# Two plain float32 products in place of nine bfloat16 ones as TensorE's warm-up, in a gated mix of a long convolution and an MLP

## The chip, the core and the metric

One core of a Trainium2 chip runs the whole program in one launch. The metric is the device time in microseconds (us). The kernel before takes 385.71 us, the median of three runs that lie between 385.69 and 385.95.

## What is computed

The inputs are x (2048 rows of 512), k and v of the same shape, four shift taps and a long filter of 2048 taps for each of the 512 channels, two MLP weights (512 x 1792 and 1792 x 512) and a gate vector of 512.

```python
x = A_q
g = _sigmoid((x * gate_w).sum(-1, keepdims=True))
a = _A_ref(x, A_k, A_v, A_shift_k, A_ssm_k, A_ssm_D)   # 4 taps on k, times v, 2048-tap causal convolution by FFT, + D * kv, times x
b = _B_ref(x, B_w1, B_w2)                              # relu(x @ w1) @ w2
return g * a + (1 - g) * b
```

The warm-up products are no part of this. They multiply ones by ones into a bank of PSUM that nobody reads.

## The kernel before

The MLP is done with operands that are each split into a high and a low part of the type float32r, three products for each tile (high by high, high by low, low by high). A product is 128 x 128 weights by 128 x 512 moving elements. The long convolution is done as a transform over small tiles of TensorE's array, in plain float32: `stage1` (L459) forward, `conv_mid` (L575) and `inverse` (L652) in the middle, `conv_end` (L727) last. The MLP runs in two eras of seven blocks of the hidden dimension, each over four chunks of 512 rows, and the pieces of the convolution are put between the MLP's.

Every piece of work is an operation in a list (`add`) with an engine, a rough duration, a rank and what it depends on. `Plan.order` plays the list through once, at build time, and writes the instructions in the order in which it would start them. So a duration in the list can move instructions on any engine. The hardware then runs each engine's instructions in that order, and semaphores hold an instruction until its operands are there.

The operations around the change are the first ones of the program:

- `warm` (L749 to L753) issues nine bfloat16 products of constant ones, one behind the other. In the list it is one operation of TensorE with the rank (-3,), that takes one of the eight PSUM banks ("cv") and gives it back.
- `load_first` (L317) brings the first four weight blocks in, one for each quarter k of the contraction. The block for k = 0 comes in two halves on ACT's queue (L329), is rounded to its high part by ACT (L334: `w0h_h_g`) and to its low part by DVE (L337: `w0l_l_g`). The blocks for k = 1 to 3 come on SP's queue and have L299 and L302.
- `load_x` brings the first 512 rows of x in; DVE makes the high part for k = 0 and all the low parts (`xh_h`, `xl_l`), ACT the other high parts.
- `mlp1_first` (L354) has the first real products (L362): twelve for each k, in groups that follow the order in which the operands come in. For k = 0 these are two of the high weights' first half by xh, two by xl, the same four for the second half, and four of the low weights by xh.

```python
        first = [(0, n, f) for m in range(2) for n in range(2) for f in (2 * m, 2 * m + 1)] + [(0, 2, f) for f in range(G)]
```

Of the kernel before, what the change touches and what calls it, by code (L numbers as in the profile page):

```python
# [8 lines left out]
F32 = mybir.dt.float32  # L9
# [4 lines left out]
S, D, DFF = 2048, 512, 1792  # L14
P = 128
# [51 lines left out]
def _flat(r):  # L67
    for x in r if isinstance(r, tuple) else (r,):
        yield from _flat(x) if isinstance(x, tuple) else (x,)


class Plan:
# [5 lines left out]
    def add(self, eng, dur, rank, fn, deps=(), take=(), give=(), dma=0, fifo=(), tiles=False, port=False, alt=None, pair=0, soon=False, ends=False):  # L78
        rank = tuple(_flat(rank))
        op = dict(tiles=tiles, alt=alt, port=port or eng == "POOL" and not dma, eng=eng, dur=dur, rank=rank, fn=fn, take=tuple(take), give=tuple(give), dma=dma, fifo=tuple(fifo),  # L80
                  pair=pair, soon=soon, ends=ends or soon, wait=0, next=[], asked=0.0, n=len(self.ops), rest=(), member=False)
        op["fn"] = fn if alt is None else lambda: fn(op["eng"])
        for d in deps:
            if d is not None:
                d["next"].append(op)
                op["wait"] += 1
        for q in fifo:
            self.turn.setdefault(q, []).append(op["n"])
        self.ops.append(op)
        return op  # L90
# [152 lines left out]
MM = 0.227  # L243
# [5 lines left out]
def build(tc, wf, xp, qn, kn, vn, hn, dn, sh, gw, w1, w2, cs1, ccf, cci, cib, out):  # L249
    nc = tc.nc  # L250
# [18 lines left out]
    add = plan.add  # L269
# [8 lines left out]
    def bank(key, tag="cv"):  # L278
        T[key] = pm.tile([P, D], F32, tag=tag, bufs=room0[tag], name="_".join(map(str, key)))
        return T[key]  # L280
# [467 lines left out]

    def warm():  # L749
        ps = bank(("warm",))  # L750
        one = nc.const_aps.tensor(1.0, (P, D), mybir.dt.bfloat16)
        for _ in range(WARM):
            mm(ps, one[:, :P], one, start=True, stop=True)  # L753

    w = add("PE", WARM * 2 * MM / 2, (-3,), warm, (), ["cv"], ["cv"])
    for k in range(4):
        load_x(0, 0, k, -1000 + k)
        load_first(k, -1002.5 + k)
# [59 lines left out]
PATIENCE = 0.5  # L818
BEHIND = 2
G = 4  # L820
WARM = 9
DMA_AHEAD = 2.0
DMA_RATE = 300000.0
DMA_LAG = [0.575, 0.8]
# [66 lines left out]
```

## Time and profile before

| | |
|---|---|
| median of three runs | 385.71 us |
| the profiled execution | 385.97 us |
| its span, first to last instruction | 384.2 us |
| TensorE busy | 379.8 us, 99% of the span |
| VectorE (DVE) busy | 266.7 us, 69% |
| ScalarE (ACT) busy | 128.8 us, 34% |
| mean granted TensorE clock | 0.999 |

The span is what the trace covers; the 1.77 us between it and the profiled execution's time lie outside the instructions. Times in the trace count from the span's start. In the rows PE is TensorE's products, PEld its weight loads, which run beside products, and a name such as `w0h_h_g` is a tile. A product's recorded duration is longer than the distance to the next one, since products follow each other in a pipeline: the distance from start to start is what a product costs.

### The profile page before, as it was taken

How to read it: one execution, taken by the hardware profiler on the slowest of the kernel's cores; microseconds unless marked ns; L12 is line 12 of the kernel's file. 1: busy time of each engine (PE TensorE's matmuls, PEld its weight loads, DVE VectorE, ACT ScalarE, POOL GpSimd, SP SyncE). 2: the span in 40 equal slices, each digit the busy share in tenths (PEclk: the TensorE clock that was granted, in tenths of full speed). 3: DMA queues.
4: the chain of work that ended last, by engine and by line, in shares of the span. 5: the costliest groups of instructions: out<-in, count | busy, mean ns of one | idle time of the engine just before them, and what ended most of it. 6: DMA issues, size and time to landing. Idle time of an engine off the chain costs nothing.

```text
span 384.2 us, 6567 instructions
## 1 busy us (share of the span) xinstructions
PE 379.8 (99%) x2505; PEld 273.8 (71%) x2505; DVE 266.7 (69%) x356; ACT 128.8 (34%) x242; POOL 91.5 (24%) x77
## 2 busy tenths in 40 slices
PE   9999999999999999999999999999999999999996
PEld 5888788668877788788655765565587788688684
DVE  4698999797989028114799687897872347687691
ACT  5643524573147525533224022313400333012100
POOL 0000000000000000000199968866995001000000
PEclk9999999999999999999999999999999999999999
DMA  7997893898648763589867876686460798399331
GB/s 274 368 317 255 298 351 113 293 333 323 208 121 330 295 234 109 185 296 275 285 203 238 307 265 227 241 308 232 139 204 3 241 342 320 120 325 357 117 124 56
DMA packets 43474, 92.51 MB, mean 241 GB/s; under 512 B 4625, under 2 KB 7201, under 8 KB 43442
## 3 DMA queue, kind: packets, MB, share of 16 engines
q1 hardware_dynamic: 43090, 91.77, 68.8%
q8 instruction: 20, 0.33, 0.4%
q10 hardware_dynamic: 288, 0.26, 0.2%
q14 instruction: 12, 0.10, 0.1%
q0 software_dynamic: 64, 0.05, 0.0%
HBM read 61.66 MB, written 30.41 MB: 240 GB/s over the span
## 4 chain that ended last, share of the span: by engine, by line
PE 99%; DVE 0%; DVEq 0%; issue 0%
PE m L406 14%; PE m L407 13%; PE m L408 13%; PE m L376 13%; PE m L377 12%; PE m L378 12%; PE iv L652 4%; PE f_h L575 4%; PE f_x L575 4%; PE m L362 3%; PE s1x L459 2%; PE s1h L459 2%; PE cy L727 2%; PE warm L753 1%; DVE o L677 0%; DVEq L887 0%
## 5 line engine op out<-in xcount | busy, mean ns | idle before, releaser
L623 POOL TENSOR_TENSOR p<-p,ha 128x512 f32<-128x512 f32 x32 | 41.1, 1308 | 202.2 <-DVE ha L617 201.6
L406 PE MATMUL m<-w1h_h,hh 128*128 128x512 f32 x224 | 88.7, 396 | 0.0
L407 PE MATMUL m<-w1l_l,hh 128*128 128x512 f32 x224 | 87.3, 390 | 0.0
L408 PE MATMUL m<-w1h_h,hl 128*128 128x512 f32 x224 | 87.2, 389 | 0.0
L389 ACT ACTIVATE hh<-m 128x512 fp32r<-128x512 f32 x56 | 33.1, 598 | 126.4 <-PE m L378 122.1
L392 DVE SCALAR_TENSOR_TENSOR hl<-m,hh 128x512 fp32r<-128x512 f32 x56 | 38.3, 688 | 44.5 <-ACT hh L389 44.3
L376 PE MATMUL m<-xh_h,w0h_h 128*128 128x512 f32 x160 | 63.0, 394 | 0.0
L377 PE MATMUL m<-xl_l,w0h_h 128*128 128x512 f32 x160 | 62.3, 390 | 0.0
L378 PE MATMUL m<-xh_h,w0l_l 128*128 128x512 f32 x160 | 62.3, 389 | 0.0
L406 PEld LDWEIGHTS m<-w1h_h,hh 128*128 128x128 f32 x224 | 42.0, 188 | 19.1 <-ACT ev L464 6.5
L408 PEld LDWEIGHTS m<-w1h_h,hl 128*128 128x128 f32 x224 | 42.0, 188 | 9.0
L407 PEld LDWEIGHTS m<-w1l_l,hh 128*128 128x128 f32 x224 | 42.1, 188 | 8.3
L376 PEld LDWEIGHTS m<-xh_h,w0h_h 128*128 128x128 f32 x160 | 30.0, 188 | 11.1 <-issue 4.2
L378 PEld LDWEIGHTS m<-xh_h,w0l_l 128*128 128x128 f32 x160 | 30.0, 188 | 6.4
L377 PEld LDWEIGHTS m<-xl_l,w0h_h 128*128 128x128 f32 x160 | 30.0, 188 | 6.0
L518 DVE TENSOR_TENSOR acc<-acc,tmp 128x1024 f32<-128x1024 f32 x24 | 29.3, 1222 | 0.6
L302 DVE TENSOR_TENSOR w1l_l<-raw,w1h_h 128x512 fp32r<-128x512 f32 x14 | 9.4, 686 | 17.7 <-ACT w1h_h L299 17.7
L662 ACT COPY bv<-iv 128x512 f32<-128x512 f32 x16 | 8.7, 589 | 37.1 <-PE iv L652 31.9
L515 DVE TENSOR_TENSOR tmp<-in,sht_sht 128x512 f32<-128x512 f32 x32 | 20.8, 685 | 0.1
L623 POOL TENSOR_TENSOR p<-p,qa 128x512 f32<-128x512 f32 x16 | 20.7, 1317 | 0.0
L617 DVE TENSOR_TENSOR ha<-f_x,ha 128x1024 f32<-128x1024 f32 x16 | 19.5, 1221 | 1.3 <-DVE qb L617 0.5
L623 POOL TENSOR_TENSOR p<-p,qb 128x512 f32<-128x512 f32 x16 | 20.3, 1290 | 0.0
(72 smaller groups left out, 468.1 us busy)
## 6 DMA issues: line engine op xcount, KB each, us to landing
sa<-ev SPq DMA_DIRECT2D x64, 256.0 KB, 3.0
sb<-bv SPq DMA_DIRECT2D x32, 256.0 KB, 3.4
br<-sb SPq DMA_DIRECT2D x16, 512.0 KB, 6.8
raw<-xp SPq DMA_DIRECT2D x28, 256.0 KB, 4.2
raw<-w SPq DMA_DIRECT2D x24, 256.0 KB, 3.8
r_x<-sa SPq DMA_DIRECT2D x12, 512.0 KB, 5.1
in<-kn SPq DMA_DIRECT2D x10, 512.0 KB, 5.0
r_h<-sa SPq DMA_DIRECT2D x10, 512.0 KB, 6.3
```

The costliest lines, as they stand in the source:

```text
L376: mm(ps, part("h", f, k), T["x", "h", xe, c, k], start=k == 0, stop=False)
L377: mm(ps, part("h", f, k), T["x", "l", xe, c, k], start=False, stop=False)
L378: mm(ps, part("l", f, k), T["x", "h", xe, c, k], start=False, stop=k == 3)
L389: nc.scalar.activation(tile_of(("hh", era, c, f), "hh", dt=F32R, p=mp, bufs=HB), T["m1", era, c, f], AF.Relu)
L392: nc.vector.scalar_tensor_tensor(tile_of(("hl", era, c, f), "hl", dt=F32R, p=mp, bufs=HB), T["m1", era, c, f], 0.0, T["hh", era, c, f].bit ...
L406: mm(ps, T["hh", era, c, f][:, z], T["w", "h", 1, f], start=f == fs[0], stop=False)
L407: mm(ps, T["hh", era, c, f][:, z], T["w", "l", 1, f], start=False, stop=False)
L408: mm(ps, T["hl", era, c, f][:, z], T["w", "h", 1, f], start=False, stop=f == fs[-1])
L515: nc.vector.tensor_tensor(o[:, z], T["k", c + (j == 0) + part][:, u], T["sht",][:, j * D:(j + 1) * D], op=OP.mult)
L518: nc.vector.tensor_tensor(T["acc", c], T["acc", c], T[dst], op=OP.add)
L575: mm(ps[b][32 * j:32 * j + 32, :], T[k("cf")][at, 64 * j + 32 * o:64 * j + 32 * o + 32], T[k("r", t, j // 2)][at, (j % 2) * D:(j % 2 + 1) ...
L623: nc.gpsimd.tensor_tensor(planes("p", dst, n), planes("p", dst, n), planes(src, u, n), op=OP.add if sign > 0 else OP.subtract)
```

## The change

The constant that is multiplied is of float32 instead of bfloat16, the number of products goes from nine to two, and the duration in the list of operations is adapted to that.

```diff
     def warm():
         ps = bank(("warm",))
-        one = nc.const_aps.tensor(1.0, (P, D), mybir.dt.bfloat16)
+        one = nc.const_aps.tensor(1.0, (P, D), F32)
         for _ in range(WARM):
             mm(ps, one[:, :P], one, start=True, stop=True)
 
-    w = add("PE", WARM * 2 * MM / 2, (-3,), warm, (), ["cv"], ["cv"])
+    w = add("PE", WARM * 4 * MM, (-3,), warm, (), ["cv"], ["cv"])
...
-WARM = 9
+WARM = 2
```

TensorE's first rows of the program before, from the last of its nine warm-up pairs on (the eight pairs ahead of it read alike; m is a PSUM tile, xh_h and xl_l the parts of x, w0h_h_g the high part of the first weights, the number at a name's end counts tiles):

```order
L753 LDWEIGHTS const-bfloat16-1.0
L753 MATMUL warm<-const-bfloat16-1.0 128x512
L362 MATMUL m_0_0_0_108<-xh_h_0_0_100,w0h_h_g_93 128x512
L362 MATMUL m_0_0_1_110<-xh_h_0_0_100,w0h_h_g_93 128x512
L362 MATMUL m_0_0_0_108<-xl_l_0_0_104,w0h_h_g_93 128x512
L362 MATMUL m_0_0_1_110<-xl_l_0_0_104,w0h_h_g_93 128x512
L362 MATMUL m_0_0_2_122<-xh_h_0_0_100,w0h_h_g_93 128x512
L362 MATMUL m_0_0_3_124<-xh_h_0_0_100,w0h_h_g_93 128x512
```

The same place of the changed program:

```order
L753 MATMUL warm<-const-float32-1.0 128x512 x2
L362 MATMUL m_0_0_0_101<-xh_h_0_0_93,w0h_h_g_86 128x512
L362 MATMUL m_0_0_1_103<-xh_h_0_0_93,w0h_h_g_86 128x512
L362 MATMUL m_0_0_0_101<-xl_l_0_0_97,w0h_h_g_86 128x512
L362 MATMUL m_0_0_1_103<-xl_l_0_0_97,w0h_h_g_86 128x512
L362 MATMUL m_0_0_2_115<-xh_h_0_0_93,w0h_h_g_86 128x512
L362 MATMUL m_0_0_3_117<-xh_h_0_0_93,w0h_h_g_86 128x512
```

Eighteen rows of the warm-up have become one row that stands for two products; the real products behind them stand as they stood. On ACT, which makes the high weights that these products wait for, the first rows of the program before are:

```order
L329 DMA ev_g_84<-wf 128x256 x2
L334 ACT_TABLE_LOAD
L334 CAST w0h_h_g_93<-ev_g_84 128x256 x2
L299 CAST xh_h_0_1_106<-raw_0_1_89 128x512
L299 CAST w0h_h_g_117<-ev_g_91 128x512
```

And of the changed program:

```order
L329 DMA ev_g_77<-wf 128x256 x2
L334 ACT_TABLE_LOAD
L334 CAST w0h_h_g_86<-ev_g_77 128x256 x2
L299 CAST xh_h_0_1_99<-raw_0_1_82 128x512
L299 CAST w0h_h_g_110<-ev_g_84 128x512
```

Nothing but the counting numbers differs there, which are lower by seven since seven products fewer were numbered. So it is over the whole program: on ACT, DVE, POOL and SP every row stands where it stood, and on TensorE every row but those of the warm-up.

## Rows read from the trace of the kernel before

**Rows 1.** The page: span, busy time, granted clock in 40 equal slices.

```profile
span 384.2 us, 6567 instructions
...
PE 379.8 (99%) x2505; PEld 273.8 (71%) x2505; DVE 266.7 (69%) x356; ACT 128.8 (34%) x242; POOL 91.5 (24%) x77
...
PEclk9999999999999999999999999999999999999999
```

**Rows 2.** The page: the chain of waits that ended last, by engine and line.

```profile
PE 99%; DVE 0%; DVEq 0%; issue 0%
PE m L406 14%; PE m L407 13%; PE m L408 13%; PE m L376 13%; PE m L377 12%; PE m L378 12%; PE iv L652 4%; PE f_h L575 4%; PE f_x L575 4%; PE m L362 3%; PE s1x L459 2%; PE s1h L459 2%; PE cy L727 2%; PE warm L753 1%; DVE o L677 0%; DVEq L887 0%
```

**Rows 3.** Timeline of the opening: start us, us, engine, line, operation [idle before].

```profile
0.75 0.14 PEld L753 LDWEIGHTS <-const-bfloat16-1.0 128*128 128x128 bf16 x2 [0.75 <-issue]
0.78 3.95 PE L753 MATMUL warm<-const-bfloat16-1.0 128*128 128x512 bf16 x9 [0.78 <-PEq L884]
1.16 0.15 PEld L753 LDWEIGHTS <-const-bfloat16-1.0 128*128 128x128 bf16 x1 [0.27 <-issue]
...
3.72 0.15 PEld L753 LDWEIGHTS <-const-bfloat16-1.0 128*128 128x128 bf16 x1 [0.27 <-issue]
...
3.85 0.41 ACT L334 CAST w0h_h_g<-ev_g 128x256 fp32r<-128x256 f32 x1 [0.91 <-DMA ev_g<-wf]
4.14 0.69 DVE L302 TENSOR_TENSOR xl_l<-raw,xh_h 128x512 fp32r<-128x512 f32 x1
4.31 0.45 PEld L362 LDWEIGHTS m<-xh_h,w0h_h_g 128*128 128x128 f32 x2 [0.43 <-ACT w0h_h_g L334]
4.31 0.89 PE L362 MATMUL m<-xh_h,w0h_h_g 128*128 128x512 f32 x2
...
4.88 0.34 PEld L362 LDWEIGHTS m<-xl_l,w0h_h_g 128*128 128x128 f32 x2
```

**Rows 4.** The same timeline, from the second group of real products on.

```profile
5.04 0.64 PE L362 MATMUL m<-xl_l,w0h_h_g 128*128 128x512 f32 x2
...
6.46 1.08 PE L362 MATMUL m<-xh_h,w0l_l_g 128*128 128x512 f32 x4
6.75 0.62 ACT L299 CAST w0h_h_g<-ev_g 128x512 fp32r<-128x512 f32 x1 [0.98 <-DMA ev_g<-wf]
...
7.43 0.76 PEld L362 LDWEIGHTS m<-xh_h,w0h_h_g 128*128 128x128 f32 x4 [0.33 <-ACT w0h_h_g L299]
...
8.46 1.08 PE L362 MATMUL m<-xl_l,w0h_h_g 128*128 128x512 f32 x4
...
9.38 1.08 PE L362 MATMUL m<-xh_h,w0l_l_g 128*128 128x512 f32 x4
```

**Rows 5.** By source line, L753 and L362: ns min/median/max, first and last start.

```profile
L753 PE MATMUL warm<-const-bfloat16-1.0 x9: 586/634/634, 0.8 to 4.1; 128*128 128x512 bf16 x9
...
L362 PEld LDWEIGHTS m<-xh_h,w0h_h_g x16: 186/188/289, 4.3 to 13.5; 128*128 128x128 f32 x16
```

**Rows 6.** Windows: each engine's busy us; the last three columns PEclk, DMA share, GB/s.

```profile
2.00:3.00 1.00, 1.00 (x4) 0.44 (x3) 0.00 (x0) 0.94 (x1) 0.00 (x0) 1.00 0.85 313
...
383.00:384.00 1.00, 0.00 (x0) 0.00 (x0) 0.00 (x0) 0.00 (x0) 0.00 (x0) 0.72 0.00 0
```

**Rows 7.** The chain of waits, in order of time: pieces from 183 us on.

```profile
183.25 0.23 PE m L378
183.47 1.88 PE f_h L575 x32
185.35 1.72 PE f_x L575 x32
187.07 0.43 PE m L376
187.50 0.24 PE m L377
```

**Rows 8.** By source line, L575: plain float32 on small tiles of the array.

```profile
L575 PE MATMUL f_x<-r_x,cf x192: 589/589/589, 185.1 to 277.1; 64*32 64x512 f32 x192
```

## The prediction

> **What bounds the kernel now.** I read the page first: TensorE is busy for 379.8 of 384.2 us [rows 1], so next to nothing but TensorE can matter. The chain of waits says the same thing from the other end: 99% of the path that ends last is TensorE, and the warm-up has 1% of it [rows 2]. Hence a microsecond that TensorE loses in the opening, and that no later wait swallows, is a microsecond of the result. The question is therefore only what TensorE does in its first 8 us, and for that I read the timeline.
>
> The reader is to see three things there. First, the warm-up starts at 0.78 us and its nine products stand 0.427 us apart (weight loads from 1.16 to 3.72 us: six steps in 2.56 us) [rows 3]. 512 columns in 0.427 us are 1.2 GHz, the lower of the clock's two levels. From 8.46 us on, four real products of 512 columns take 0.92 us, 0.229 each [rows 4], which is the upper level, 2.4 GHz, with a little on top. The column of the granted clock does not show this: it reads 1.00 in the warm-up too [rows 6], while it does show the fall after the last product (0.72 in the last whole microsecond). So the level in the opening must be read from the distances.
>
> Second, when the level changed. Two rows give it. The ninth warm-up product lasts 0.586 us where the others last 0.634 [rows 5]: 0.048 shorter. At the lower level throughout, its stream would end at 0.78 + 9 x 0.427 = 4.62 us; it ended at 4.57, and since what is left halves at the upper level, the change came 0.096 before 4.62, at 4.52 us. And the first real weight load, at 4.31 us, lasts 0.289 us where the others last 0.188 [rows 3, 5]; at half clock it would last 0.376, so x + (1 - x/0.376) x 0.188 = 0.289 gives x = 0.20, that is 4.51 us. I take 4.52. TensorE had streamed bfloat16 products without a gap from 0.78 us until then.
>
> Third, what the real products wait for. The first pair is held until ACT has the first half of the high weights, at 3.85 + 0.41 = 4.26 us. The next pair needs xl_l, which DVE has at 4.14 + 0.69 = 4.83 us; its weights are loaded from 4.88 us [rows 3]. From 5.04 to 7.37 us ten products run in file (six at 0.237, four at 0.228) [rows 4]. Then k = 1 begins: its weights can only be loaded at 7.43 us, since ACT has them at 6.75 + 0.62 = 7.37 us, and ACT had sat idle for 0.98 us before that, waiting for the DMA of that block [rows 4]. The next group starts at 8.46 us, so the first group of k = 1 streams from 8.46 - 0.92 = 7.54 us. TensorE loses about 0.17 us at 7.4 us, and what it waits for there is a transfer that SP issued, not its own work.
>
> **The change part by part.** The order of all engines is as it was but for the warm-up itself, so no transfer, cast or wait moves; the planner's other duration comes to nothing. What is left are three terms.
>
> *The length of the warm-up.* The trace before has plain float32 on small tiles: 32 records in 1.72 us [rows 7]. Each record uses a tile of 64 rows by 32 columns [rows 8], so eight lie side by side on the array and 32 records are four after another, 0.43 us each; and since the code writes 16 products there (`rounds` for two values of o, eight each), a product is two records. A plain float32 product thus costs 0.86 us at the upper level, 1.72 at the lower, and two of them 3.44 us. Nine at 0.427 cost 3.84. Against that stands a longer first weight load: a float32r one at the lower level is 0.376 by the row above, a bfloat16 one 0.14, so 0.23 us more. The warm-up then ends at 0.78 + 0.23 + 3.44 = 4.45 us instead of 4.57: **0.12 us earlier**. Bounds: from 0.35 earlier (the first load is no longer than before) to the case that each record's load lies bare, three more loads of 0.376, 1.01 us later. I take the first estimate, since in every row of the opening loads lie under products (steps of 0.427 and 0.228 with loads of 0.15 and 0.19).
>
> [...]
>
> *What an earlier end brings.* The first pair would start at 4.45 instead of 4.57 us, and run at the lower level until the change. If that still comes at 4.52 us, the pair ends near 4.94 us; the pair behind it waits for its weight load, which can't start before 4.88 us and lasts 0.19. So the second pair starts at 5.07 us at the best, as before. And were k = 0 done sooner, k = 1 would still wait for ACT until 7.43 us. **Gain: 0.** The cover is DVE's xl_l first and the transfer of the weights for k = 1 second; together they also hide a delay of about 0.13 + 0.17 = 0.3 us.
>
> *The clock.* The warm-up's purpose lies in the level at which the first twelve products run. If plain float32 raises it as bfloat16 did, by the time the real products run in file, this term is 0. For it: plain float32 has the array to itself from 183.47 to 187.07 us and the products behind it run at 0.24 us again [rows 7], so it holds the upper level at least; and TensorE has no gap between warm-up and real work (4.45 against a load that may start at 4.31). Against it: holding is not raising, those rows have eight tiles side by side, and no row shows plain float32 on the full array. I take 0, and price the other case below. If the rise follows the start of the stream, it is later by the 0.23 us of the first load, at 4.75 us, which costs half of that, 0.12 us, under a cover of 0.3.
>
> The sum is 0 +- 0.1 against the profiled execution's 385.97 us. That execution lies 0.26 above the median, so I forecast the median: **385.7 us**, own range 385.4 to 386.2. A change under 0.2%, 0.77 us, can't be told from none with this kernel.
>
> **The rivals.** *A. Plain float32 does not raise the clock, or not in time (slower).* The one lapse that the rows show between the start of a gapless stream and the upper level is 4.52 - 0.78 = 3.74 us; I use it as a price and claim no more. Counted from the first real product, at 4.45, the rise is at 8.19 us. Until then 3.74 / 0.44 = 8.5 products are done (0.427 to 0.455 each); the other 3.5 take 0.8 us, so k = 0 ends at 8.99 instead of leaving TensorE free for k = 1 at 7.54: +1.45 us, **387.2 us**. In general a rise at T costs about (T - 4.52)/2 - 0.3, which passes 0.77 us at T = 6.7; from there it decides. For it: on the full array plain float32 is untried, and it takes four times as long for its 512 columns as bfloat16 (1.72 against 0.43 us), so whatever is counted may come in more thinly. Against it: the rows of the convolution. [...]
>
> *B. The weight loads lie bare (a little slower).* The warm-up ends at 4.45 + 1.13 = 5.58 us, twelve products at 0.232 follow until 8.36, and k = 1 begins 0.82 us late: **386.5 us**, at the edge of what can be told. The steps in rows 3 and 4 speak against it.
>
> *C. The earlier end reaches the result (faster).* It would need the second pair and k = 1 not to wait for DVE and for the transfer; the most is the 0.35 us of the bound above, **385.35 us**, within 0.2%.
>
> **How the numbers follow.** Forecast 0.65; A 0.27, of which 0.04 with a rise before 6.7 us, which is hidden or too small to tell; B 0.04, half of it under the bound; C and an unseen gain 0.04. Slower is 0.23 + 0.02 = 0.25; same 0.65 + 0.04 + 0.02 = 0.71; faster 0.04 (an unseen gain alone). The range reaches from C to A: 385.3 to 387.2 us.
>
> **What would show it.** In the changed profile: four warm-up records 0.85 us apart; the first real product's start near 4.4 us; weight loads for xl_l at 4.88 us and for k = 1 at 7.43 us, where they were; products 0.24 us apart from 5.04 us. If they are 0.43 apart there, and the group that started at 8.46 us starts near 9.9, it is A. If the warm-up's records lie 1.1 us or more apart, it is B. The forecast is wrong if the clock's rise is past 6.7 us, or if an engine that I took as unmoved is late in the opening.

## The result and the profile after

The changed kernel takes 386.41 us (median of 22 runs, 385.62 to 388.05), the kernel before 385.88 beside it (22 runs, 385.61 to 386.60). The ratio is 1.0016, with a 95% interval of 1.0009 to 1.0022. So the change costs about 0.5 us: less than the 0.77 us that I had set as the bound of what can be told, but with 22 runs of each it is told. The forecast was no change, and a step of it is wrong.

Besides the median, look at the scatter. Each run comes with its time and its span, and the difference, the time outside the span, is what the trace's instructions don't cover. For the kernel before it is 1.72 to 1.92 us in every one of the 82 runs whose span is on record (those beside the experiments; the 22 above have times alone). For the changed kernel (33 runs, with the repetition below) it is 1.72 to 3.05, above 1.92 in 18 of them. The means, in us:

| | runs | time | span | outside the span |
|---|---|---|---|---|
| before | 82 | 385.94 | 384.16 | 1.78 |
| changed | 33 | 386.43 | 384.30 | 2.13 |

0.35 of the 0.49 us lie outside the span; the 0.14 inside can't be told from the scatter of the spans (standard deviations 0.32 and 0.38, so 0.14 +- 0.15 at 95%).

The opening in the trace after, against [rows 3] and [rows 4] (timeline: start us, us, engine, line, operation):

```profile
0.75 0.50 PEld L753 LDWEIGHTS warm<-const-float32-1.0 128*128 128x128 f32 x2 [0.75 <-issue]
0.78 3.52 PE L753 MATMUL warm<-const-float32-1.0 128*128 128x512 f32 x4 [0.78 <-PEq L884]
...
1.77 0.34 PEld L753 LDWEIGHTS warm<-const-float32-1.0 128*128 128x128 f32 x1 [0.52 <-issue]
...
2.62 0.34 PEld L753 LDWEIGHTS warm<-const-float32-1.0 128*128 128x128 f32 x1 [0.52 <-issue]
...
4.25 0.30 PEld L362 LDWEIGHTS m<-xh_h,w0h_h_g 128*128 128x128 f32 x2 [1.29 <-ACT w0h_h_g L334]
4.25 0.73 PE L362 MATMUL m<-xh_h,w0h_h_g 128*128 128x512 f32 x2
...
4.82 0.30 PEld L362 LDWEIGHTS m<-xl_l,w0h_h_g 128*128 128x128 f32 x2 [0.28 <-DVE xl_l L302]
...
5.66 0.30 PEld L362 LDWEIGHTS m<-xh_h,w0h_h_g 128*128 128x128 f32 x2 [0.54 <-ACT w0h_h_g L334]
...
7.61 1.07 PE L362 MATMUL m<-xh_h,w0h_h_g 128*128 128x512 f32 x4
...
8.51 1.07 PE L362 MATMUL m<-xl_l,w0h_h_g 128*128 128x512 f32 x4
```

Two plain float32 products are four records, 0.85 us apart from the second on, and TensorE is done with them when the first real weights come, at 4.25 us. The second pair still waits for DVE's xl_l (the release is named in the row). The third, at 5.66 us, then stands 0.54 us for the second half of the high weights, a wait that the forecast did not have, and the group that started at 8.46 us before starts at 8.51. In this execution the clock is at its upper level when the first real weights are loaded: two loads take 0.30 us together, against 0.45 in [rows 3].

What differs lies elsewhere. The page's line of queue q8, of the kind "instruction" (queue, kind: packets, MB, share; I take it that it loads TensorE's code, since TensorE's program is the longest), reads for the kernel before:

```profile
q8 instruction: 20, 0.33, 0.4%
```

and for the changed kernel, with its line of the engines' busy time and instructions:

```profile
PE 379.5 (99%) x2500; PEld 273.5 (71%) x2500; DVE 266.4 (69%) x356; ACT 128.5 (33%) x242; POOL 91.4 (24%) x77
...
q8 instruction: 19, 0.31, 0.4%
```

Twenty blocks of 0.016 MB against nineteen, within the span. For the changed kernel the transfers behind the end of its span, 384.0 us, are these (stretch from 383.9 to 388.5 us in forty slices of 0.115 us):

```profile
GB/s 0 0 0 0 0 0 0 0 0 0 0 142 0 0 0 0 0 0 0 0 0 0 0 0 0 0 0 0 0 0 0 0 0 0 0 0 0 0 0 0
DMA packets 1, 0.02 MB, mean 4 GB/s; under 512 B 0, under 2 KB 0, under 8 KB 0
...
q8 instruction: 1, 0.02, 1.4%
```

The twentieth block is there, but it moves at about 385.2 us, over 1 us after the last instruction. In the kernel before it moved at about 375 us (stretch from 370 to 384 us in slices of 0.35 us; the lone 47 GB/s is it, 0.016 MB in 0.35 us, between stores of results):

```profile
GB/s 392 316 0 0 0 0 0 99 404 246 0 0 0 0 47 0 0 0 0 0 0 246 427 76 0 0 0 0 0 0 0 0 0 0 287 220 243 0 0 0
...
q8 instruction: 1, 0.02, 0.5%
```

The number of TensorE's instructions has changed with the warm-up: the page counts 2505 products and 2505 loads before [rows 1], and 2500 of each after. That gave the theory "code": the program is ten instructions shorter, and its end now falls so that the last block comes only after all work is done, and the execution waits for it. Its rivals, "clock" in what follows, were a later or more variable rise of the clock, by the length of the warm-up or by its type.

### The profile page after: what moved, and what is told of

It is laid out like the page before. It is cut to its first block, busy times and chain, and to the rows that moved or that the text cites. A ratio compares the mean times of both kernels' runs of the same rounds, so it can differ in the third digit from the quotient of the medians.

```text
span 384.0 us, 6557 instructions
## 1 busy us (share of the span) xinstructions
PE 379.5 (99%) x2500; PEld 273.5 (71%) x2500; DVE 266.4 (69%) x356; ACT 128.5 (33%) x242; POOL 91.4 (24%) x77
## 4 chain that ended last, share of the span: by engine, by line
PE 98%; DMA 1%; DVE 0%; ACTq 0%; ACT 0%; DVEq 0%; issue 0%
PE m L406 14%; PE m L407 13%; PE m L408 13%; PE m L376 13%; PE m L377 12%; PE m L378 12%; PE iv L652 4%; PE f_h L575 4%; PE f_x L575 4%; PE m L362 3%; PE s1x L459 2%; PE cy L727 2%; PE s1h L459 2%; DMA ev_g<-wf 1%; DVE o L677 0%; ACTq L329 0%
```

## The experiments

In the kernels with another warm-up, the warm-up's duration in the planner's list was kept as before, so that no other instruction moves.

**The kernel before, and the changed kernel, once more.**

> The kernel before itself, as a control, so that the spans and granted clocks of single executions stand beside each other. Every theory expects a ratio of 1.000 and times of 385.6 to 386.6 us. If its executions scatter as widely as those of the changed kernel did (385.62 to 388.05 us), the loss of 0.16% is scatter of the machine and not of the change.

> The changed kernel again: a median of about 386.4 us, +0.1 to +0.2%, if the loss is real. Theory 'moment of the rise': its executions scatter over 385.6 to 388 us, since the rise of the clock falls before the first real product in some and after it in others. Theory 'constant cost' (some piece of the opening is always dearer): they scatter no more than those of the kernel before and all lie 0.5 us higher.

Before: 385.79 us against 385.85 (ratio 0.9998, 0.9989 to 1.0007), outside the span 1.73 to 1.89 in all 11 runs. Changed: 386.22 us (1.0008, 0.9999 to 1.0017), outside the span up to 2.93, above 1.92 in 5 of 11. By the medians alone these 11 runs don't tell the loss (the interval just includes 1), but the scatter outside the span is back, in the changed kernel and not in the kernel before. So it is not a constant cost, and most of it is not inside the span: the medians of the spans are 383.9 and 384.1. The opening of the profiled execution of this repetition also shows what a late rise is (timeline, TensorE alone):

```profile
4.33 1.22 PE L362 MATMUL m<-xh_h,w0h_h_g 128*128 128x512 f32 x2
5.35 1.05 PE L362 MATMUL m<-xl_l,w0h_h_g 128*128 128x512 f32 x2
6.20 0.78 PE L362 MATMUL m<-xh_h,w0h_h_g 128*128 128x512 f32 x2
6.82 0.62 PE L362 MATMUL m<-xl_l,w0h_h_g 128*128 128x512 f32 x2
7.28 1.09 PE L362 MATMUL m<-xh_h,w0l_l_g 128*128 128x512 f32 x4
8.20 1.07 PE L362 MATMUL m<-xh_h,w0h_h_g 128*128 128x512 f32 x4
```

Products are 0.43 us apart (the lower level) from 5.35 to 6.20 us, and 0.23 apart (the upper) from 6.82. k = 1 begins at 8.20 us instead of 7.61 in the run above. So the rise, before 4.25 us there and after 6.20 here, moves by about 2 us or more from one execution to the next, with the same program.

**The type of the warm-up against its length.** First eight bfloat16 products instead of the nine of before, then two float32 products and one of bfloat16:

```diff
-        for _ in range(WARM):
+        for _ in range(8):
```

> Eight bfloat16 products instead of nine: a warm-up of 8 x 0.427 = 3.42 us, as long as that of two plain float32 products (4 x 0.853 = 3.41), but of the old type. Theory 'length': it behaves as the changed kernel, median 386.3 to 386.5 us with the same wide scatter. Theory 'type' (plain float32 counts for less with the clock): it behaves as the kernel before, 385.8 to 385.9 us.

```diff
+        two = nc.const_aps.tensor(1.0, (P, D), F32)
+        for _ in range(2):
+            mm(ps, two[:, :P], two, start=True, stop=True)
         one = nc.const_aps.tensor(1.0, (P, D), mybir.dt.bfloat16)
-        for _ in range(WARM):
+        for _ in range(1):
             mm(ps, one[:, :P], one, start=True, stop=True)
```

> Two plain float32 products and one bfloat16 product behind them: 3.84 us, as long as the nine bfloat16 ones. Theory 'length': it behaves as the kernel before, 385.8 to 385.9 us and little scatter. Theory 'type': it stays at about 386.4 us, since the float32 part is what is missing to the clock.

Eight bfloat16 products: 385.83 us (1.0001, 0.9992 to 1.0010), outside the span 1.73 to 1.81. Two float32 and one bfloat16: 386.16 us (1.0009, 0.9999 to 1.0019), outside the span above 1.92 in 6 of 11. By my expectations this speaks for the type. But the two kernels also differ in another thing: the first has two instructions fewer than before, the second eight. The spans have nearly the same median, 384.1 and 384.0. The next four kernels part type and count.

**The count of instructions restored.** The changed kernel, with five tiny products behind its last real one (shown without the warm-up's own lines, which are two float32 products as in the changed kernel):

```diff
...
+        tail = bank(("tail",))
+        some = nc.const_aps.tensor(1.0, (P, D), mybir.dt.bfloat16)
+        for _ in range(5):
+            mm(tail[:, :1], some[:, :P], some[:, :1], start=True, stop=True)
     phase(0)
```

> The changed kernel with five bfloat16 products of a single column each behind the last real product, into a bank that nobody reads: TensorE's program has as many instructions again as the kernel before (nine fewer products, five more here, of two each, and two plain float32 ones that become four each). Theory 'code': most of the loss lies behind the last instruction, in the loading of a block of TensorE's code that the shorter program asks for too late; then the time outside the span is back at 1.72 to 1.92 us in every execution, and the median at 385.9 to 386.0 us. Theory 'clock' (all of the loss comes from a later rise in the opening): nothing changes, 386.2 to 386.4 us and up to 3 us outside the span.

385.92 us (1.0005, 0.9997 to 1.0014), outside the span 1.72 to 1.91 in all 11 runs. The page counts 2505 products again and twenty blocks within the span:

```profile
PE 380.2 (99%) x2505; PEld 274.5 (71%) x2505; DVE 266.9 (69%) x356; ACT 129.2 (34%) x242; POOL 91.5 (24%) x77
...
q8 instruction: 20, 0.33, 0.3%
```

Five products that compute nothing, at the very end, take the time outside the span away. "Clock" could not bring that about.

**A shorter program without any float32.** The kernel before, with five products instead of nine:

```diff
-        for _ in range(WARM):
+        for _ in range(5):
```

> Five bfloat16 products instead of nine: no plain float32 at all, but TensorE's program is shorter by eight instructions, as it is with two plain float32 products and one bfloat16 one. Theory 'code': the time outside the span is over 1.9 us in about half of the executions, as with float32. Theory 'type': it stays at 1.72 to 1.92 us. The span also shows what a warm-up of 2.1 us costs in the opening: by my formula for a late rise at most 1.5 us, under 0.3 us if the real products that follow at 4.3 us count in time.

388.00 us (1.0050, 1.0035 to 1.0064; six runs). Outside the span 1.90 to 2.24 us, above 1.92 in 5 of 6, with nothing but bfloat16 in the warm-up; the last block moves behind the end of the span of 386.6 us (stretch from 386 to 391 us in slices of 0.125 us):

```profile
GB/s 0 0 0 0 0 0 0 0 0 0 0 0 0 0 131 0 0 0 0 0 0 0 0 0 0 0 0 0 0 0 0 0 0 0 0 0 0 0 0 0
...
q8 instruction: 1, 0.02, 1.2%
```

The opening cost more than I had allowed (mean span 385.90, 1.74 above before, for a bound of 1.5): the first real products, at 4.55 us after a gap of 1.48, are still 0.43 us apart when k = 1 begins (timeline, TensorE alone):

```profile
4.55 1.22 PE L362 MATMUL m<-xh_h,w0h_h_g 128*128 128x512 f32 x2 [1.48 <-ACT w0h_h_g L334]
...
8.13 1.91 PE L362 MATMUL m<-xh_h,w0l_l_g 128*128 128x512 f32 x4
9.84 1.45 PE L362 MATMUL m<-xh_h,w0h_h_g 128*128 128x512 f32 x4
11.12 1.09 PE L362 MATMUL m<-xl_l,w0h_h_g 128*128 128x512 f32 x4
```

**The old warm-up with a shorter program.** To leave the opening as it was, I took the ten instructions from the end instead: five products of the last tile of the MLP's second layer, with their weight loads, are left out.

```diff
-                mm(ps, T["hl", era, c, f][:, z], T["w", "h", 1, f], start=False, stop=f == fs[-1])
+                if (era, c, s) != (1, CHUNKS[1][-1], 3) or f not in fs[1:6]:
+                    mm(ps, T["hl", era, c, f][:, z], T["w", "h", 1, f], start=False, stop=f == fs[-1])
```

> The warm-up of before, nine bfloat16 products, but five of the low-part products are left out of the last tile of the MLP's second layer, so that TensorE's program is as much shorter (ten instructions) as in the changed kernel. Part of the computation is left out: the last 128 rows of one chunk miss five of their seven low-part terms. The span must be shorter by 5 x 0.2275 = 1.14 us, 382.7 to 383.7 us. Theory 'code': the time outside the span is over 1.9 us in about half of the executions, up to 3 us, with a warm-up that is untouched. Theory 'type': it stays at 1.72 to 1.92 us, median 384.7 us in all.

384.93 us (0.9977, 0.9968 to 0.9986). The spans are 382.6 to 383.6, shorter by the five products as expected. Outside the span it is up to 2.91, above 1.92 in 4 of 11, and the last block again comes behind the end of the span, 382.8 us (the same stretch as above, from 383.9 us on):

```profile
GB/s 142 0 0 0 0 0 0 0 0 0 0 0 0 0 0 0 0 0 0 0 0 0 0 0 0 0 0 0 0 0 0 0 0 0 0 0 0 0 0 0
...
q8 instruction: 1, 0.02, 1.6%
```

With the warm-up untouched, the shorter program alone brings the effect.

**Where the edge is.** The same tail as above, with two products instead of five.

> The changed kernel with two products of one column behind the last real product, so that TensorE's program is six instructions shorter than before instead of ten. It is to bracket the edge: at eight fewer the time outside the span is longer in half of the executions, at two fewer it is not. Theory 'code' has no say on which side six lies, but asks for one or the other: either all executions at 1.72 to 1.92 us, or half of them above. Values between, with a smaller excess in all, would speak against an edge.

385.86 us (1.0006, 0.9995 to 1.0016), but outside the span above 1.92 in 5 of 11, up to 2.81: six fewer is on the side of the short programs, and a tail of tiny products as such does not take the effect away. The median of the times hides it, since just under half of the runs are touched. The edge lies between six and two instructions fewer than before. Over all kernels: with six to ten instructions fewer, 38 of 72 runs lie above 1.92 us; with two fewer, as many as before, or more, none of 112.

The moment of the last block jumps too. With two fewer it moves at about 375 us, as in the kernel before; with six to ten fewer it moves behind the span or is not recorded at all. Yet ten instructions are not much of TensorE's time: with five products and their loads left out at the end, the mean span is 1.1 us shorter. What makes the block jump by 10 us no row shows.

**The clock by itself.** The kernel before with eight float32 products as its warm-up, and with 32 of bfloat16:

```diff
-        one = nc.const_aps.tensor(1.0, (P, D), mybir.dt.bfloat16)
-        for _ in range(WARM):
-            mm(ps, one[:, :P], one, start=True, stop=True)
...
+        two = nc.const_aps.tensor(1.0, (P, D), F32)
+        for _ in range(8):
+            mm(ps, two[:, :P], two, start=True, stop=True)
```

> A long warm-up of eight plain float32 products, 13.65 us at the lower clock: the opening has no cover left, and the end of the warm-up is at 0.78 + 13.65 - (13.65 - (T - 0.78))/2 us, so every microsecond of the rise T costs half a microsecond. Theory 'plain float32 raises the clock as well as bfloat16': the same median as with 32 bfloat16 products, about 390.5 us. Theory 'counts for less': later by half of the difference of the rises, 0.2 to 1.2 us. Never raised at all: 395.4 us.

```diff
-        for _ in range(WARM):
+        for _ in range(32):
```

> The same with 32 bfloat16 products, 32 x 0.427 = 13.65 us at the lower clock. With a rise at 4.5 us the warm-up ends at 9.5 us and the result is about 390.5 us; its scatter over executions is half the scatter of the rise. Both theories agree on this one; it is what the eight plain float32 products are set against.

391.20 us (1.0134, 1.0121 to 1.0147) and 391.19 us (1.0137, 1.0124 to 1.0150), four runs each: the type makes no difference that four runs can show (the times of one kernel scatter by up to 1.3 us), and "never raised", 395.4 us, is out. The weight loads of the eight float32 products show the rise itself, with no other work on TensorE yet (timeline, weight loads):

```profile
5.18 0.34 PEld L753 LDWEIGHTS warm<-const-float32-1.0 128*128 128x128 f32 x1 [0.52 <-issue]
6.03 0.34 PEld L753 LDWEIGHTS warm<-const-float32-1.0 128*128 128x128 f32 x1 [0.52 <-issue]
6.80 0.19 PEld L753 LDWEIGHTS warm<-const-float32-1.0 128*128 128x128 f32 x1 [0.43 <-issue]
7.23 0.19 PEld L753 LDWEIGHTS warm<-const-float32-1.0 128*128 128x128 f32 x1 [0.24 <-issue]
```

From 0.85 us apart to 0.43, and from 0.34 us to 0.19: the change comes between 6.03 and 6.80 us. With 32 bfloat16 products it comes late as well in the execution that was profiled:

```profile
6.28 0.15 PEld L753 LDWEIGHTS <-const-bfloat16-1.0 128*128 128x128 bf16 x1 [0.27 <-issue]
6.68 3.60 PEld L753 LDWEIGHTS <-const-bfloat16-1.0 128*128 128x128 bf16 x17 [0.25 <-issue]
```

Both kernels were 0.7 us above my 390.5, since I had put the rise at 4.5 us and it came later, by about 2 us in the two executions that were profiled.

## Why the prediction failed, point by point

**What bounds the kernel** was right, and so was what the first real products wait for: DVE's xl_l is named as the second pair's release after, too.

**The step that failed** is the sentence "The order of all engines is as it was but for the warm-up itself, so no transfer, cast or wait moves", and with it "What is left are three terms". I counted the transfers that the program issues, and not those that load the program. The change takes ten instructions from TensorE (18 of bfloat16 go, 8 of float32 come), and the runs show that this costs the 0.35 of the 0.49 us that lie outside the span: five empty products at the end take it away, and ten instructions fewer bring it with the old warm-up. That it goes by the last block of code, which moves at 385.2 us instead of 375, is inferred from its moment. In what I had were TensorE's 2505 products and 2505 loads [rows 1], 5010 instructions, and the page's twenty blocks for them; no row told me on which side of an edge the program ends.

The trace has blocks of 0.016 MB (0.33 MB in 20, 0.31 in 19). How many instructions a block holds no run shows; 5010 in twenty blocks are about 250 each or a little more, an estimate, and at 250 the 5000 of the changed kernel fill twenty too. So the estimate shows no edge between the two.

**The base.** I forecast from the median of three runs, 385.71 us; over 22 runs the same kernel has 385.88. So 0.18 of the 0.71 us between forecast and result are the base, and 0.53 the change.

**The length of the warm-up** was right in its main part: 0.85 us a record. The first record takes 0.99 us to the next (0.78 to 1.77), so a first load does cost something, 0.13 us, and less than the 0.23 that I added (the real weights' loads last up to 0.333 us in the repetition, not the estimated 0.376). In the repetition, where the rise came late, the first real products start at 4.33 us, against my 4.45. It changed nothing in the sum.

**What an earlier end brings**: nothing that shows, as forecast: 8.51 us against 8.46 in the two profiles. But the cover was in part another one than I named: the third pair's wait for the second half of the high weights held TensorE in the profile after, and k = 1, at 7.61 us, waited for nothing.

**The clock.** That plain float32 raises it, the first choice, held: in the profile after, nothing but plain float32 had run on TensorE when it rose, before 4.25 us. That it does so as bfloat16 does is what the pair of long warm-ups shows within its scatter, 391.20 against 391.19 us. In that pair the number of products made no difference that shows: 8 and 32 products of the same length in all (16 records x 0.853 us and 32 x 0.427 at the lower level), and a rise between 6.03 and 6.80 us and between 6.28 and 6.68 us. What the rise waits for was not shown.

The two levels themselves show as steps in these two traces: 0.85 us and then 0.43 for a float32 record, 0.427 us and then about 0.22 for a bfloat16 product (17 weight loads in 3.60 us, sixteen steps and a load). The 1.2 and 2.4 GHz of the prediction take a column as one clock, which was my estimate and no run shows; 512 bfloat16 columns pass at 1.2 and at about 2.3 columns a nanosecond.

My 4.52 us for the moment of the rise came out near, but not by its working. The second real load, at 4.57 us, lasts 0.19 us in the kernel before, so the level changed about there; the two rows that I used don't show it by themselves. In the repetition the first real load lasts 0.286 us, as long as the 0.289 that I read as a change of level, though the clock rose after 6.20 us there. And the first warm-up product of the kernel before lasts 0.586 us like the ninth, at the lower level. Its step to the second is 0.38 us (0.78 to 1.16) and not 0.427, so the stream ends at 4.57 us without any rise (by source line, ns min/median/max, first and last start; the first row is from the repetition, the second from the kernel before):

```profile
L362 PEld LDWEIGHTS m<-xh_h,w0h_h_g x1: 286/286/286, 4.3 to 4.3; 128*128 128x128 f32 x1
...
L753 PE MATMUL warm<-const-bfloat16-1.0 x1: 586/586/586, 0.8 to 0.8; 128*128 128x512 bf16 x1
```

I also treated the moment as fixed. In the profiles of the changed kernel it is before 4.25 and between 6.20 and 6.82 us. The price that I set for a late rise, half of the delay less 0.3 us, held: k = 1 begins 0.66 us after my 7.54 in the repetition, and a rise at 6.5 us costs 0.69 by it. Whether the scatter of the kernel before, 385.54 to 386.73 us, comes from this isn't shown: in both of its profiles products are 0.24 us apart from 5.1 us on. The three runs that I had, 385.69 to 385.95, did not show that scatter, and my bound of the measurable came from them.

**Rival A** (float32 doesn't raise the clock, or not in time) fell in its first half by the eight float32 products. A late rise does come in some executions, and the runs don't show that it comes more often after float32. **Rival B** (bare weight loads) fell by the 0.85 us of the records, **rival C** (a gain) by the median.

**What stays open.** Whether the 0.14 us inside the span are real. Why a short program costs between nothing and 1.3 us, and nothing in about half of the executions. That the execution waits for the block is inferred from the kernels in which both come and go together; no row shows the wait itself, and single executions agree only in part. Of the six profiled ones with six to ten instructions fewer, four have the late block, with 1.90 to 2.16 us outside the span; in two no twentieth block is recorded, with 2.03 us (the repetition of the changed kernel) and 1.81 us (six fewer).

## What to carry to other kernels

A change that "moves nothing" can still change the length of an engine's program, here from 5010 products and loads to 5000. When a time moves by a tenth of a per cent and the spans do not, compare the time outside the span, run by run, and look in the queues of the kind "instruction" for a block that lands after the last instruction, as at 385.2 us here; a few empty products at the end, five here, tell whether the program's length is the cause. And look at how an effect is distributed: here the medians of two kernels on the same side of the edge were 385.86 and 386.41 us.

## What was not expected of the hardware

Six to ten instructions fewer cost up to 1.3 us outside of all work, in about half of the executions (38 of 72). And the same program, the changed kernel, has its clock's rise before 4.25 us after the span's start in one execution and after 6.20 us in another. A long warm-up of bfloat16 also had it past 6 us (between 6.28 and 6.68), so a late rise is not float32's alone.
